# Two activation biases as immediates in place of a column in SBUF (mLSTM, then two expert layers, one core)

## The chip, the core and the metric

The kernel runs on one core of a Trainium2 chip. The metric is the device time of one execution in microseconds (us): the median of three runs of the kernel before is 632.94 us. The core has a matrix engine (TensorE, PE in the profile; its weight loads are PEld), VectorE (DVE), ScalarE (ACT), GpSimd (POOL) and SyncE (SP), which issues the DMAs. Each engine works through its own queue in order, and semaphores hold an instruction until what it reads or overwrites is ready.

## The reference

Three stages follow each other, all in float32:

```python
# 1: mLSTM, 2 batches x 8 heads, 768 steps, head size 40 (gated, stabilised recurrence)
x = y.transpose(0, 2, 1, 3).reshape(1536, 320)
# 2: layer one, 320 -> 2048 -> 320
h = x @ w_in
g = h - np.tanh(h)
x = g @ w_out
# 3: layer two, four experts, 320 -> 1024 -> 320
p = domain_probs / (domain_probs.sum(-1, keepdims=True) + 1e-9)
out = sum(p[:, e:e+1] * (np.maximum(x @ w1[e], 0) @ w2[e]) for e in range(4))
```

## The kernel before

The recurrence is computed in six chunks of 128 steps for each of the two batches, as masked score matrices. Chunk after chunk feeds layer one, whose weights arrive as 64-bit words and are converted on the chip (conv). Matrices are split in a high and a low part, so that products of float32 precision are made of several matmuls: an input product of layer one is 16 matmuls of 256 columns (L679), an output product 12 matmuls of 320 columns (L729).

Layer one has 48 steps i. Step i makes a 128 x 512 block of h in a PSUM bank (in1, mm_in), applies the activation to it (hidden1) and multiplies it into the output (out1). hidden1 is a list of eight pieces, put at different places of the order of work:

- sq: Tanh (L689) and Square (L690), both from PSUM, into t and z;
- sq2: s = (z + GA)^2 (L694), with the bias GA read from column 0 of the tile ga;
- shrink: t = h - tanh(h) on DVE (L697);
- poly: two DVE instructions (L700, L701), a polynomial in z for small h, which needs s;
- small: z = Relu(T2 - z) (L704), with T2 read from column 1 of ga; it is non-zero where h is small;
- pick: a predicated copy on DVE (L707), which takes the polynomial where z is non-zero and is the last reader of the PSUM bank;
- high (ACT, L711) and low (POOL, L715): the split of the result for the output matmuls.

Each piece runs once in a step, so L694 and L704 run 48 times each, all on 128 x 512.

The order of work is written by hand: every piece of work has a key, and run() issues the pieces by rising key. Step i of layer one has keys from 4i on. For keys under 95 (the cut, a little before step 24) only the queues of TensorE and SyncE are held to that order:

```python
with tc.manual_schedule(engines={nc.tensor.engine, nc.sync.engine}):
    ...
    run(-99, P["cut"])
with tc.manual_schedule():
    run(P["cut"], 9999)
```

There a planner, which gives instructions prices of its own, sets the order on ACT, DVE and POOL. From key 95 on all five engines keep the written order. The first 23 steps share ACT with the recurrence (att_exp, L374: eight exponentials for each chunk and batch) and the weight conversion (L189, L212). From the second half of layer one on, layer two's weights and inputs are prepared as well (conv_q, L238 to L265, and build, whose pieces are L545 to L654); layer two itself is steps of key 192 + 8m, with matmuls L671 and L729.

The tile ga is [128, 24], allocated among the constants and filled at the start by two memsets on DVE (L760, L762); between them stands the memset of gap (L761), and the first scan of the gates comes behind them on DVE.

Of the kernel before, what the change touches and what calls it, by code (L numbers as in the profile page):

```python
# [7 lines left out]
F32 = mybir.dt.float32  # L8
# [3 lines left out]
ACT = mybir.ActivationFunctionType  # L12
# [86 lines left out]
T2 = 0.0625  # L99
GA = -1.2788529396057129  # L100
# [5 lines left out]
def kernel(  # L106
# [14 lines left out]
    nc = tc.nc  # L121
    const = ctx.enter_context(tc.tile_pool(name="const", bufs=1))
# [11 lines left out]
        return ps.tile([128, 512], F32, tag=f"b{i}", name=f"b{i}")  # L134

    ident = const.tile([128, 128], F32, name="ident")
    ga = const.tile([128, 24], F32, name="ga")
    xT = [xpool.tile([128, 5, 512], F32R, tag=f"xT{i}", name=f"xT{i}") for i in range(NJ // 2)]
    gap = xpool.tile([128, 16], F32, tag="gap", name="gap")
    acc = const.tile([128, NTT, DM], F32, name="acc")  # L140
# [198 lines left out]
    def att_load(j, b):  # L339
        a = att.setdefault((j, b), {})  # L340
        a["kq"] = at.tile([128, 2, 4, 128], F32, tag="kq", name="kq")
        nc.sync.dma_start(out=a["kq"], in_=kq[j, b])

    def att_kv(j, b):
        a = att[j, b]
        a["kv"] = at.tile([128, KW + H * DV], F32, tag="kv", name="kv")
        nc.sync.dma_start(out=a["kv"], in_=kv[j, b])
# [30 lines left out]
    def first_rows(b, g):  # L378
        h = slice(4 * g, 4 * g + 4)
        nc.vector.tensor_tensor(  # L380
            out=blk[b][32:48, h, :], in0=blk[b][0:16, h, :],
            in1=g_t[:, 0:128].unsqueeze(1).to_broadcast([16, 4, 128]), op=ALU.mult,
        )

    def first_late(b, g):
        p = att.setdefault((0, b), {})["e", g] = bank(2 * b + g)
        nc.tensor.matmul(p, ident, late.unsqueeze(1).to_broadcast([128, 4, 128]), start=True, stop=False)

    def first_sum(b, g):
        nc.tensor.matmul(  # L390
            att[0, b]["e", g], rows, blk[b][:, 4 * g:4 * g + 4, :].rearrange("p h t -> p (h t)"), start=False, stop=True
        )
# [28 lines left out]
    def att_s(j, b):  # L421
        t = att[j, b]["kq"]
        ps = [abank() if j else bank(4 + 2 * b + g) for g in range(2)]
        for h in range(4):
            for g in range(2):
                nc.tensor.matmul(
                    ps[g][:, h * 128:(h + 1) * 128], t[64 * g:64 * g + PK, 0, h, :], t[64 * g:64 * g + PK, 1, h, :],
                    start=True, stop=True,
                )
        for g in range(2):  # L430
            att[j, b]["s", g] = ps[g]
# [251 lines left out]
    def hidden1(hp):  # L683
        v = {}

        def sq():
            v["z"] = ew.tile([128, 512], F32, tag="z", name="z")
            v["t"] = ew.tile([128, 512], F32, tag="t", name="t")
            nc.scalar.activation(out=v["t"], in_=hp, func=ACT.Tanh)  # L689
            nc.scalar.activation(out=v["z"], in_=hp, func=ACT.Square)  # L690

        def sq2():
            v["s"] = ew.tile([128, 512], F32, tag="s", name="s")
            nc.scalar.activation(out=v["s"], in_=v["z"], func=ACT.Square, bias=ga[:, 0:1])  # L694

        def shrink():
            nc.vector.tensor_tensor(out=v["t"], in0=hp, in1=v["t"], op=ALU.subtract)  # L697

        def poly():
            nc.vector.scalar_tensor_tensor(out=hp, in0=v["s"], scalar=GB, in1=hp, op0=ALU.add, op1=ALU.mult)  # L700
            nc.vector.scalar_tensor_tensor(out=hp, in0=hp, scalar=GC, in1=v["z"], op0=ALU.mult, op1=ALU.mult)  # L701

        def small():
            nc.scalar.activation(out=v["z"], in_=v["z"], func=ACT.Relu, scale=-1.0, bias=ga[:, 1:2])  # L704

        def pick():
            nc.vector.copy_predicated(v["t"], v["z"].bitcast(I32), hp)  # L707

        def high():
            v["gh"] = gp.tile([128, 512], F32R, tag="gh", name="gh")  # L710
            nc.scalar.activation(out=v["gh"], in_=v["t"], func=ACT.Copy)  # L711

        def low():
            v["gl"] = gp.tile([128, 512], F32R, tag="gl", name="gl")
            nc.gpsimd.tensor_tensor(out=v["gl"], in0=v["t"], in1=v["gh"].bitcast(F32), op=ALU.subtract)  # L715

        return v, (sq, sq2, shrink, poly, small, pick, high, low)

    def block2(src, tag):
# [13 lines left out]
    with tc.manual_schedule():  # L733
        nc.sync.dma_start(out=f_t, in_=fg)
        nc.sync.dma_start(out=i_t, in_=ig)
        for b in range(B):
            nc.sync.dma_start(out=blk[b][0:32], in_=c_blk[:, 8 * b:8 * b + 8])
        att_load(0, 0)
        att_load(0, 1)
        att_kv(0, 0)  # L740
        att_kv(0, 1)
        c_i0 = conv("i", 0, 0), conv("i", 0, 1)
        c_i1 = conv("i", 1)
        for f in range(2):
            c_i0[f][0]()
        nc.sync.dma_start(out=acc[:, 0:6, :], in_=og[:, 0:6, :])
        nc.sync.dma_start(out=sel, in_=c_sel)
        nc.vector.memset(late, 0.0)
        nc.gpsimd.memset(ident, 0.0)
        nc.gpsimd.affine_select(  # L750
            out=ident, in_=ident, pattern=[[-1, 128]], compare_op=ALU.not_equal, fill=1.0, base=0, channel_multiplier=1
        )
        nc.gpsimd.affine_select(
            out=late, in_=late, pattern=[[1, 128]], compare_op=ALU.is_ge, fill=NEG, base=0, channel_multiplier=-1
        )
        nc.vector.memset(rows, 0.0)
        nc.vector.memset(rows[32:48], 1.0)
        for b in range(B):
            nc.vector.memset(blk[b][32:64], 0.0)
        nc.vector.memset(ga[:, 0:1], GA)  # L760
        nc.vector.memset(gap, 0.0)  # L761
        nc.vector.memset(ga[:, 1:2], T2)  # L762
        nc.gpsimd.memset(rst, 1.0)
        nc.gpsimd.memset(rst.rearrange("p (j t) -> p j t", t=128)[:, :, 0:1], 0.0)
        for b in range(B):
            nc.gpsimd.memset(st[b], 0.0)
        nc.gpsimd.memset(egb, 0.0)
        for b, g in ((0, 0), (0, 1), (1, 0)):
            first_late(b, g)
        scan_m, log_f, log_f2, scan_g, log_i, log_i2 = gates(0, 128)  # L770
        scan_m()
        log_f()
        log_i(nc.gpsimd)
        log_f2()
        scan_g()
        log_i2(nc.vector, rows[0:16])
        for b in range(B):
            for g in range(2):
                first_rows(b, g)
        att_s(0, 0)  # L780
        for g in range(2):
            first_sum(0, g)
            first_exp(0, g)
            att_k(0, 0, (g,))
        scan_m, log_f, log_f2, scan_g, log_i, log_i2 = gates(128, S)
        scan_m()
        log_f()
        first_sum(1, 0)
        first_exp(1, 0)
        att_s(0, 1)  # L790
        att_k(0, 1, (0,))
        att_a(0, 0, 0)
        log_f2()
        att_a(0, 0, 1)
        scan_g()
        nc.sync.dma_start(out=g_d, in_=g_t)
        c_i1[0]()
        for b in range(B):
            att_gb(1, b)
        att_load(1, 0)  # L800
        att_kv(1, 0)
        c_i0[0][1]()
        c_i0[1][1]()
        first_late(1, 1)
        first_sum(1, 1)
        first_exp(1, 1)
        att_k(0, 1, (1,))
        att_a(0, 1, 0)
        c_i0[0][2]()
        c_i0[0][3]()  # L810
        att_a(0, 1, 1)
        nc.scalar.activation(out=acc[:, 0:2, :], in_=acc[:, 0:2, :], func=ACT.Sigmoid)
        c_i0[0][4]()
        nc.scalar.activation(out=acc[:, 2:6, :], in_=acc[:, 2:6, :], func=ACT.Sigmoid)
        log_i(nc.gpsimd)
        for b in range(B):
            for g in range(2):
                att_h(0, b, g)
        c_i0[1][2]()
        att_den(0, 0)  # L820
        att_gate(0, 0, nc.gpsimd)
        log_i2(nc.gpsimd)
        c_i0[1][3]()
        c_i0[1][4]()
        c_i0[0][5]()
        att_u(0, 0)
        att_x(0, 0)
        att_den(0, 1)
        att_gate(0, 1, nc.vector)
        growth()  # L830
        c_i1[1]()
        x_tr(0)
        x_split(0)
        att_x(0, 1)
        att_u(0, 1)
        biases()
        x_tr(1)
        c_i0[1][5]()
        x_split(1)
        att_mask(1, 0)  # L840
        att_mask(1, 1)
        for b in range(B):
            att_st(0, b)
        c_i2, c_o0, c_i3, c_o1 = conv("i", 2), conv("o", 0), conv("i", 3), conv("o", 1)
        c_i2[0]()
        att_load(1, 1)
        att_kv(1, 1)
        att_eg(1)
        c_o0[0]()
# [304 lines left out]
```

## Time and profile before

| | |
|---|---|
| three runs, us | 632.07, 632.94, 633.74 (median 632.94) |
| span of the profiled execution, us | 633.0 (no other time of this execution is given) |
| PE busy, us | 597.6 (94% of the span) |
| PEld busy, us | 579.7 (92%) |
| DVE busy, us | 476.4 (75%) |
| ACT busy, us | 353.1 (56%) |
| POOL busy, us | 336.6 (53%) |

The span goes from the first to the last instruction of one profiled execution. Busy time is the time in which an engine has an instruction in work; instructions of one engine overlap by a little, so the distance between two starts (the pitch) is shorter than a duration. The matrix engine's clock is given as the granted share of its full speed, 2.4 GHz: 1.00 is that level, 0.50 is 1.2 GHz.

### The profile page before, as it was taken

The page shows a single profiled execution, that of the slowest core. Times are in us where ns is not written, and L with a number is a line of the kernel's source. Part 1 is how long each engine was busy: PE and PEld are TensorE (multiplying, and loading weights), DVE is VectorE, ACT ScalarE, POOL GpSimd, SP SyncE. Part 2 cuts the span into 40 slices and gives each one's busy share as a digit, 9 for nine tenths or more (in the row PEclk, how much of TensorE's full clock was granted, in tenths as well). Part 3 has the DMA queues.
Part 4 walks back from the last instruction along what each step waited for, and adds up shares of the span by engine and source line. Part 5 has one row for each costly group of instructions (what it writes and reads, how often), then busy time and mean ns, then how long its engine had stood idle before and what let it go on. Part 6 is the DMA issues. An engine that isn't in the chain of part 4 may idle for free.

```text
span 633.0 us, 12023 instructions
## 1 busy us (share of the span) xinstructions
PE 597.6 (94%) x4505; PEld 579.7 (92%) x4505; DVE 476.4 (75%) x1011; ACT 353.1 (56%) x738; POOL 336.6 (53%) x329
## 2 busy tenths in 40 slices
PE   8695899999989999899898999999999999999997
PEld 4595899999988999898888999999999999999997
DVE  8978968899686879985777766676676766666675
ACT  3687498776788997786544454223542234432221
POOL 4666857775348876669748684304844046530000
PEclk9586798999999999999998999999999999999999
DMA  7945863743010110003000130101211011201011
GB/s 252 311 131 160 312 193 111 244 174 120 2 42 23 56 55 2 1 1 88 22 3 1 33 109 22 55 1 35 76 55 55 2 35 55 76 2 42 1 43 41
DMA packets 29602, 48.15 MB, mean 76 GB/s; under 512 B 2264, under 2 KB 20056, under 8 KB 29544
## 3 DMA queue, kind: packets, MB, share of 16 engines
q1 hardware_dynamic: 29544, 47.39, 23.2%
q8 instruction: 35, 0.57, 0.4%
q14 instruction: 23, 0.19, 0.1%
HBM read 45.31 MB, written 2.06 MB: 75 GB/s over the span
## 4 chain that ended last, share of the span: by engine, by line
PE 54%; DVE 8%; ACT 5%; issue 2%; POOL 1%; DVEq 0%; ACTq 0%; POOLq 0%
PE b L729 27%; PE b L671 23%; PE b L679 3%; DVE t L707 1%; DVE xo L638 1%; DVE t L697 1%; DVE b L987 1%; DVE s L987 1%; ACT z L690 1%; ACT gh L711 1%; POOL gl L715 1%; DVE gh L722 1%; ACT gh L721 1%; ACT z L704 1%; ACT t L689 1%
## 5 line engine op out<-in xcount | busy, mean ns | idle before, releaser
L729 PE MATMUL b<-wo,gh 128*128 128x320 f32 x960 | 201.8, 310 | 2.3 <-DVE acc L874 1.3
L729 PE MATMUL b<-wo,gl 128*128 128x320 f32 x768 | 168.4, 311 | 2.4 <-POOL gl L715 2.3
L729 PEld LDWEIGHTS b<-wo,gh 128*128 128x128 f32 x960 | 149.8, 189 | 3.4 <-ACT so L645 1.5
L729 PEld LDWEIGHTS b<-wo,gl 128*128 128x128 f32 x768 | 123.6, 190 | 3.9 <-POOL gl L715 3.9
L679 PE MATMUL b<-xT,wi 128*128 128x256 f32 x768 | 106.7, 292 | 8.9 <-ACT wi L212 4.2
L679 PEld LDWEIGHTS b<-xT,wi 128*128 128x128 f32 x768 | 99.0, 198 | 11.1 <-ACT wi L212 4.4
L721 ACT ACTIVATE gh<-b 128x256 fp32r<-128x256 f32 x96 | 36.9, 384 | 121.6 <-DVE b L987 71.0
L715 POOL TENSOR_TENSOR gl<-t,gh 128x512 fp32r<-128x512 f32 x48 | 63.1, 1314 | 57.1 <-ACT gh L711 43.6
L671 PE MATMUL b<-so,wt 128*128 128x256 f32 x560 | 90.7, 284 | 1.4 <-DVE gl L722 0.8
L987 DVE TENSOR_TENSOR b<-b,s 128x256 f32<-128x256 f32 x192 | 81.2, 423 | 2.4 <-ACT s L991 2.4
L671 PEld LDWEIGHTS b<-so,wt 128*128 128x128 f32 x560 | 80.0, 189 | 2.8 <-DVE gl L722 1.6
L721 ACT ACTIVATE gl<-b 128x256 fp32r<-128x256 f32 x96 | 36.8, 384 | 81.0 <-DVE b L987 80.9
L246 POOL TENSOR_TENSOR wb<-raw,wb 128x384 fp32r<-128x384 f32 (+1 forms) x32 | 32.6, 1018 | 82.8 <-ACT wb L238 81.3
L722 DVE SCALAR_TENSOR_TENSOR gh<-b,gh 128x256 fp32r<-128x256 f32 x96 | 40.7, 424 | 47.6 <-ACT gh L721 47.6
L722 DVE SCALAR_TENSOR_TENSOR gl<-b,gl 128x256 fp32r<-128x256 f32 x96 | 40.7, 424 | 46.0 <-ACT gl L721 46.0
L987 DVE TENSOR_TENSOR s<-b,s 128x256 f32<-128x256 f32 x144 | 58.4, 418 | 9.3 <-PE b L671 5.0
L671 PE MATMUL b<-xo,wb 128*128 128x256 f32 x400 | 65.1, 280 | 0.1
L671 PEld LDWEIGHTS b<-xo,wb 128*128 128x128 f32 x400 | 57.8, 189 | 0.4 <-DVE gl L722 0.4
L246 POOL TENSOR_TENSOR wt<-tf,wt 128x512 fp32r<-128x512 f32 (+1 forms) x32 | 41.4, 1294 | 7.5 <-ACT wt L265 5.9
L704 ACT ACTIVATE z<-z,ga 128x512 f32<-128x512 f32 x48 | 34.7, 723 | 18.9 <-DVE b L701 12.1
L697 DVE TENSOR_TENSOR t<-b,t 128x512 f32<-128x512 f32 x48 | 32.9, 686 | 15.1 <-ACT z L690 11.7
L711 ACT ACTIVATE gh<-t 128x512 fp32r<-128x512 f32 x48 | 30.3, 631 | 20.1 <-DVE t L707 19.3
(132 smaller groups left out, 1030.2 us busy)
## 6 DMA issues: line engine op xcount, KB each, us to landing
kq<-in_kq_dram SPq DMA_DIRECT2D x12, 512.0 KB
raw<-in_wb_dram SPq DMA_DIRECT2D x16, 384.0 KB
raw<-in_wa_dram SPq DMA_DIRECT2D x7, 768.0 KB
w<-g_d SPq DMA_DIRECT2D x10, 512.0 KB
raw<-in_wa_dram SPq DMA_DIRECT2D x8, 640.0 KB
raw<-in_wb_dram SPq DMA_DIRECT2D x16, 320.0 KB
kv<-in_kv_dram SPq DMA_DIRECT2D x12, 372.0 KB
raw<-in_wb_dram SPq DMA_DIRECT2D x16, 128.0 KB
```

The lines of the kernel that those rows point to most:

```text
L246: nc.gpsimd.tensor_tensor(out=o[r, k], in0=i[r, :, q], in1=o[r, 2 * q].bitcast(F32), op=ALU.subtract)
L638: nc.vector.tensor_tensor(out=o1()[r, :, 2, sl], in0=v["o"][r, 1], in1=o1()[r, :, 2, sl].bitcast(F32), op=sub)
L671: nc.tensor.matmul(o[:, 0:256], w[:, kw, b if b < 3 else b - 3], x_op(t, a, kx), start=(i == 0), stop=(i == 3),)
L679: nc.tensor.matmul(hp[:, c0:c0 + w], w_in(n, lo, kt, f), xt[:, xk, x0:x0 + w], start=(i == 0), stop=(i == 7))
L697: nc.vector.tensor_tensor(out=v["t"], in0=hp, in1=v["t"], op=ALU.subtract)
L704: nc.scalar.activation(out=v["z"], in_=v["z"], func=ACT.Relu, scale=-1.0, bias=ga[:, 1:2])
L711: nc.scalar.activation(out=v["gh"], in_=v["t"], func=ACT.Copy)
L715: nc.gpsimd.tensor_tensor(out=v["gl"], in0=v["t"], in1=v["gh"].bitcast(F32), op=ALU.subtract)
L721: nc.scalar.activation(out=g[:, 0], in_=src, func=ACT.Relu)
L722: nc.vector.scalar_tensor_tensor(out=g[:, 1], in0=src, scalar=0.0, in1=g[:, 0].bitcast(F32), op0=ALU.max, op1=ALU.subtract)
L729: nc.tensor.matmul(o[:, 0:DM], g[a][:, c:c + 128], w_out(n, lo, f), start=(first and i == 0), stop=(last and i == 2))
L987: nc.vector.tensor_tensor(out=out, in0=x, in1=y, op=ALU.add)
```

## The change

The two biases are given to the activation instructions as numbers. Nothing reads ga any more; its tile stays, named pad, and one memset of its 24 columns takes the place of the two memsets of single columns.

```diff
-    ga = const.tile([128, 24], F32, name="ga")
+    ga = const.tile([128, 24], F32, name="pad")
...
-            nc.scalar.activation(out=v["s"], in_=v["z"], func=ACT.Square, bias=ga[:, 0:1])
+            nc.scalar.activation(out=v["s"], in_=v["z"], func=ACT.Square, bias=GA)
...
-            nc.scalar.activation(out=v["z"], in_=v["z"], func=ACT.Relu, scale=-1.0, bias=ga[:, 1:2])
+            nc.scalar.activation(out=v["z"], in_=v["z"], func=ACT.Relu, scale=-1.0, bias=T2)
...
-        nc.vector.memset(ga[:, 0:1], GA)
         nc.vector.memset(gap, 0.0)
-        nc.vector.memset(ga[:, 1:2], T2)
+        nc.vector.memset(ga, 0.0)
```

## Rows read from the trace of the kernel before

**Rows 1.** The page, busy us, share of the span and instructions of each engine.
```profile
PE 597.6 (94%) x4505; PEld 579.7 (92%) x4505; DVE 476.4 (75%) x1011; ACT 353.1 (56%) x738; POOL 336.6 (53%) x329
```

**Rows 2.** Busy time by stretch; behind POOL: granted clock, DMA share, GB/s.
```profile
80.00:100.00 20.00, 18.69 (x147) 18.22 (x146) 14.20 (x32) 19.95 (x41) 11.47 (x12) 0.91 0.69 217
100.00:120.00 20.00, 20.00 (x175) 19.69 (x174) 15.02 (x33) 14.88 (x33) 16.30 (x17) 1.00 0.48 172
...
400.00:420.00 20.00, 20.00 (x155) 20.00 (x154) 13.84 (x36) 5.07 (x15) 1.41 (x2) 1.00 0.01 3
```

**Rows 3.** Groups of instructions on ACT: shapes and count, busy us, mean ns, idle before.
```profile
L704 ACT ACTIVATE z<-z,ga 128x512 f32<-128x512 f32 x48 | 34.7, 723 | 18.9 <-DVE b L701 12.1 <-DVE den L475 3.7 <-DVE den L476 3.0
L694 ACT ACTIVATE s<-z,ga 128x512 f32<-128x512 f32 x48 | 34.7, 723 | 0.3
L711 ACT ACTIVATE gh<-t 128x512 fp32r<-128x512 f32 x48 | 30.3, 631 | 20.1 <-DVE t L707 19.3 <-DVE den L475 0.9
L690 ACT ACTIVATE z<-b 128x512 f32<-128x512 f32 x48 | 28.4, 592 | 0.0
```

**Rows 4.** The timeline of ACT, 212 to 234 us: start, duration, instruction, [idle before].
```profile
212.19 0.63 ACT L711 ACTIVATE gh<-t 128x512 fp32r<-128x512 f32 x1 [0.27 <-DVE t L707]
212.72 0.58 ACT L689 ACTIVATE t<-b 128x512 f32<-128x512 f32 x1
...
213.68 0.72 ACT L704 ACTIVATE z<-z,ga 128x512 f32<-128x512 f32 x1
214.29 0.72 ACT L694 ACTIVATE s<-z,ga 128x512 f32<-128x512 f32 x1
...
228.79 0.44 ACT L545 ACTIVATE xm<-acc 128x256 f32<-128x256 f32 x1
...
233.60 0.72 ACT L694 ACTIVATE s<-z,ga 128x512 f32<-128x512 f32 x1
```

**Rows 5.** The timeline of ACT, 80 to 95 us.
```profile
81.25 0.72 ACT L694 ACTIVATE s<-z,ga 128x512 f32<-128x512 f32 x1
...
93.86 0.73 ACT L704 ACTIVATE z<-z,ga 128x512 f32<-128x512 f32 x1
94.48 0.70 ACT L374 ACTIVATE w<-w,bia 128x128 f32<-128x128 f32 x2
```

**Rows 6.** The timeline of PE: the waits that the argument uses.
```profile
95.19 1.13 PE L426 MATMUL b<-kq 64*128 64x128 f32 x14 [1.31 <-ACT w L374]
96.25 3.63 PE L679 MATMUL b<-xT,wi 128*128 128x256 f32 x16
...
186.68 2.06 PE L679 MATMUL b<-xT,wi 128*128 128x256 f32 x16 [1.58 <-DVE t L707]
...
191.91 2.05 PE L679 MATMUL b<-xT,wi 128*128 128x256 f32 x16 [1.41 <-DVE t L707]
...
229.28 0.44 PE L560 MATMUL b<-ident,xm 128*128 128x128 f32 x2 [0.42 <-ACT xm L545]
```

**Rows 7.** The timeline of ACT, 182 to 188 us.
```profile
182.24 0.73 ACT L694 ACTIVATE s<-z,ga 128x512 f32<-128x512 f32 x1
...
186.83 0.71 ACT L694 ACTIVATE s<-z,ga 128x512 f32<-128x512 f32 x1
```

**Rows 8.** The timeline of DVE, 185 to 188 us.
```profile
185.80 0.74 DVE L707 COPY_PREDICATED t<-z,b 128x512 f32<-128x512 int32 x1 [0.85 <-ACT z L704]
...
187.57 0.70 DVE L700 SCALAR_TENSOR_TENSOR b<-s,b 128x512 f32<-128x512 f32 x1 [0.47 <-ACT s L694]
```

**Rows 9.** The timeline of DVE at 234 us.
```profile
234.35 0.70 DVE L700 SCALAR_TENSOR_TENSOR b<-s,b 128x512 f32<-128x512 f32 x1
```

**Rows 10.** The timeline of DVE at the start.
```profile
3.58 0.07 DVE L761 MEMSET gap<- 128x16 f32 x1
```

**Rows 11.** Busy time in two microseconds at 96, columns as in rows 2.
```profile
96.00:98.00 2.00, 2.00 (x14) 1.88 (x12) 1.93 (x5) 2.00 (x5) 0.00 (x0) 0.61 0.69 279
```

**Rows 12.** The timeline of ACT at 30 us.
```profile
30.49 2.14 ACT L374 ACTIVATE w<-w,bia 128x128 f32<-128x128 f32 x7
```

## Prediction

> **What bounds the kernel now.** I read the busy table first, then busy time by stretches of 20 us, then the chain that ended last, and last the timelines of ACT, DVE and PE around each wait of PE that the chain or the table of waits named. The busy table says that TensorE is the bound: 597.6 of 633.0 us, while ACT, the only engine that the change makes faster, is busy for 353.1 us [rows 1]. The stretches say where this is not so. From 100 to 120 us, and again in layer two at 400, PE is busy without a gap [rows 2]; there a faster ACT can give nothing by itself. From 80 to 100 us PE is busy for 18.69 of 20 us and ACT for 19.95 [rows 2]: ACT is full, and PE waits for it. The waits of PE that matter here are few: 1.31 us at 95 us for an exponential on ACT, 1.58 and 1.41 us at 186 and 191 us for the predicated copy on DVE, 0.42 us at 229 us for a small copy on ACT [rows 6]. The chain that ended last is ACT work for most of 212 to 234 us, then DVE, and from about 335 us on matmuls alone. So the question is how much of ACT's saving lies ahead of one of these waits.
>
> **What one instruction saves.** The two touched groups, 48 instructions each, take 723 ns; the activation of the same shape from SBUF without a column operand, the copy of L711, takes 631 ns [rows 3]. The difference is 92 ns. That the function makes no large difference is suggested by the Square of L690, which takes 592 ns from PSUM with its bias a constant already [rows 3]. Instructions overlap, so what the next one gains is the pitch, not the duration: after L704 at 213.68 the next starts at 214.29, 0.61 us later; after L711 at 212.19 it starts at 212.72, 0.53 us later [rows 4]. So a follower on ACT gains 0.08 us, and a DVE instruction that waits for the end gains 0.09. I use 0.088 for one and keep 0.080 and 0.092 as its ends. The whole saving of ACT is 96 x 0.092 = 8.8 us, which is the upper bound of the change; the lower bound is nothing.
>
> It could be otherwise: were the fetch of the operand hidden behind the instruction before, nothing would come closer together inside a run of activations, and each of the three runs below would gain only at its end. That is 3 x 0.09 = 0.27 us, or 632.7 us; the two pitches speak against it. The Trainium skill (ScalarE: Activation LUTs, section "What ACT_TABLE_LOAD costs") says that back-to-back activations overlap by about 93 ns and that "each `[128,1]` pointer operand adds ≈ 93 ns", which leaves open whether the one is hidden in the other. By that, the trace agrees in size (92 ns), and its pitches, 0.61 against 0.53 us, say that it is not hidden [rows 3, 4].
>
> **Which of the 96 count.** I went through the starts on ACT from 38 to 288 us.
>
> - Before 80 us there are 10. PE waits there too, but behind weight conversion on DVE, and ACT has gaps. I count none.
> - From 80 to 95 us there are 4, from 81.25 to 93.86, in an unbroken run of ACT that ends with the exponentials PE waits for [rows 5, 6]. They start 4 x 0.088 = 0.35 us earlier. PE is full behind that [rows 2], so the gain travels with it to 180 us, where DVE, and no longer PE, sets the next wait. I take 0.20 of it, with 0 and 0.37 as ends.
> - From 95 to 180 us there are 29. PE's full queue hides them. If that cover were gone they would be worth at most 29 x 0.09 = 2.6 us.
> - From 180 to 188 us there are 4, the first at 182.24 and the last at 186.83 [rows 7]. DVE's copy at 185.80 waits 0.85 us for L704, and its polynomial at 187.57 waits 0.47 us for L694 [rows 8]; these two lead to the waits of PE at 186.68 and 191.91 [rows 6]. 4 x 0.088 = 0.35 us, ends 0.32 and 0.37.
> - From 188 to 212 us there are 12. PE alternates input and output products without a gap; I count none; uncovered, they would be worth 1.1 us.
> - From 212.7 to 234.3 us there are 12, the first at 213.68 and the last at 233.60 [rows 4]. Three of them are followed by a wait of ACT for DVE and count for nothing. Seven stand ahead of the copy at 228.79 that PE waits for [rows 4, 6], and two more ahead of the polynomial at 234.35, which starts as L694 ends [rows 4, 9]. 9 x 0.088 = 0.79 us, ends 0.72 and 0.83.
> - After 234.3 us there are 25. DVE then has work without a gap up to 251 us, and after that DVE, POOL and PE hand over to each other; ACT waits for them. I count none; uncovered, they would be worth 2.3 us.
>
> The memsets at the start: two of one column go, one of 24 columns comes. The nearest row is the memset of 16 columns, 0.07 us [rows 10]. The bounds are -0.14 and +0.07 us on DVE ahead of the first scan; I take nothing. No wait is added: L694 and L704 lose an operand that was ready long before, and no transfer is moved.
>
> **The sum.** 0.20 + 0.35 + 0.79 = 1.34 us. Against the profiled execution's 633.0 this is 631.7; that execution stands 0.06 above the median of the runs, so against the median, 632.94, it is 631.6 us. With the ends of the terms it is 631.4 to 631.9. This is 0.2%, and 0.3% (1.9 us, or 631.04) is about what a measurement of this kernel can tell from no change.
>
> **The rivals.**
>
> *More than the sum.* The 16 input matmuls at 96.25 take 3.63 us against 2.05 for the same work at 191.91 [rows 6]; the granted clock in these two microseconds is 0.61 [rows 11], that is, most of them at the lower level, 1.2 GHz. It fell right behind the wait of 1.31 us. If the exponentials come earlier and this wait shrinks, the fall may not come: 1.58 us more, or 630.0 us. If the wait goes altogether, as with a happier order of the planner, it is 1.31 more, 628.7 us. For it: the fall is at this one place, and ahead of it ACT is full. Against it: the waits of 1.58 and 1.41 us at 186 and 191 us brought no fall, so a wait of this length does not always bring one; and the sum shortens the wait by 0.35 us only.
>
> *Slower.* For keys under 95 the planner orders ACT, DVE and POOL, and with other prices for 46 or so activations it may order them otherwise. The place that would hurt is the same run from 80 to 95 us. If a group of exponentials for a later chunk, seven of them being 2.14 us [rows 12], slips ahead of the ones that PE waits for at 95.19, the full queue of PE behind that passes the loss on to the end; and a wait so much longer brings a second half-speed stretch, 1.58 us. 2.14 + 1.58 - 1.34 = +2.4, or 635.3 us. It decides from a delay of 1.34 + 1.9 = 3.2 us on. For it: the order there is not written, and ACT has no room. Against it: durations that change by an eighth (92 of 723 ns) on 96 of 738 activations leave most choices alone, and PE and SP keep their order, so a later group has no inputs earlier.
>
> *Hidden.* DVE or POOL takes over as the one that ends last at 186 and from 212 on, and PE has what it needs no earlier: a gain of 0 to 0.7, or 632.2 to 632.9. Against it: at both places DVE has gaps that end with ACT [rows 8].
>
> **How the numbers follow.** The sum has a chance of 0.42, more than the sum 0.33, slower 0.15, hidden 0.07, the same pitch as before 0.02 (632.7), and 0.01 that the numbers are put into a column again when the program is built (632.9). The sum's own range, with some slack, is 630.8 to 632.4, and 0.07 of its 0.42 lies past 631.04. Faster by over 0.3%: 0.33 + 0.07 = 0.40. Slower: 0.15, and 0.02 for a fall of the clock at a place I have not seen, 0.17. The rest is 0.43. The range reaches down to 628.7, where the whole wait at 95 is gone, and up to 634.5, which is no gain at all with a second half-speed stretch (632.94 + 1.58). Below lie some 0.07, above some 0.12.
>
> **What the profile after would show.** Right: L694 and L704 at about 631 ns, ACT busy for about 344 us; the pitch behind them at 0.53 us; PE's wait at 95 us shorter by some 0.3 us, the two waits at 186 and 191 us together shorter by about as much, the start of layer one's last outputs and everything from 335 us on earlier by 1.3 us, with the matmul part of layer two as long as before. Wrong: the names of L694 or L704 still show a second input, or 723 ns stand; the order of instructions on ACT before 180 us is another one, and PE's first gap-free stretch starts at another time by more than 1 us; the clock falls in other stretches than before; or ACT's gaps grow by what its instructions lost, while PE starts each step when it did.

## The result and the profile after

The change made the kernel slower.

| | before | after |
|---|---|---|
| median, us | 633.47 (632.07 to 635.92, 6 runs) | 638.87 (635.9 to 640.31, 6 runs) |
| ratio to before, with its 95% interval | | 1.0068 [1.0046, 1.009] |
| span of the profiled execution, us | 633.0 | 634.1 |

By the ratio, which is not the quotient of the two medians (1.0085), the loss is 0.68%, 4.3 us [2.9, 5.7]; by the medians it is 5.4 us.

Two more things are needed to read this. The device time of an execution is about 1.8 us above its span (635.9 and 634.1 for the profiled execution of after), so the profile of before stands for a run of some 634.8 us and not, as the prediction had it, of 633.0. And the profiled execution of after is the shortest of its six. Its mean granted clock was 0.970; the median over the runs of after is 0.963, over the runs of before beside the experiments 0.970. So the profile below shows where PE waits, but less of the loss than a usual run has; no usual run of after was traced.

The operand itself did what was forecast. The busy table of after, beside [rows 1]:

```profile
PE 597.0 (94%) x4505; PEld 578.6 (91%) x4505; DVE 479.2 (76%) x1010; ACT 345.8 (55%) x738; POOL 336.9 (53%) x329
```

The groups of ACT in after, beside [rows 3]; the second input is gone from the names:

```profile
L694 ACT ACTIVATE s<-z 128x512 f32<-128x512 f32 x48 | 30.4, 634 | 0.3
L711 ACT ACTIVATE gh<-t 128x512 fp32r<-128x512 f32 x48 | 30.3, 632 | 27.0 <-DVE t L707 25.9 <-DVE den L474 0.9
L704 ACT ACTIVATE z<-z 128x512 f32<-128x512 f32 x48 | 30.3, 632 | 13.9 <-DVE b L701 10.8 <-DVE den L475 2.8 <-DVE den L474 0.2
```

723 ns became 632 and 634, as long as the copy without a column. The timeline of ACT in after (start, duration), beside [rows 4]:

```profile
214.15 0.63 ACT L704 ACTIVATE z<-z 128x512 f32<-128x512 f32 x1
214.67 0.63 ACT L694 ACTIVATE s<-z 128x512 f32<-128x512 f32 x1
215.19 0.74 ACT L212 ACTIVATE wo<-raw 128x640 fp32r<-128x640 f32 x1
```

The pitch behind both is 0.52 us in place of 0.61: the whole 0.09 us reaches the next instruction, so the fetch of the column was not hidden behind the instruction before it. The Trainium skill (ScalarE: Activation LUTs, section "What ACT_TABLE_LOAD costs") prices a `[128,1]` operand at about 93 ns; the 89 to 91 ns here agree, and the pitch adds that back-to-back issue does not hide it.

What went wrong is on PE, some 20 us ahead of the first place where the prediction counted a gain. The timeline of PE in after (start, duration, instruction, [idle before <- what ended it]):

```profile
64.89 1.13 PE L426 MATMUL b<-kq 64*128 64x128 f32 x14 [1.56 <-DVE xT L521]
65.94 2.15 PE L679 MATMUL b<-xT,wi 128*128 128x256 f32 x16
...
75.87 0.42 PE L450 MATMUL b<-st,kq 104*128 104x82 f32 x2 [2.29 <-DVE w L436]
...
79.01 2.05 PE L679 MATMUL b<-xT,wi 128*128 128x256 f32 x8
...
90.87 1.17 PE L679 MATMUL b<-xT,wi 128*128 128x256 f32 x8
...
96.17 1.13 PE L426 MATMUL b<-kq 64*128 64x128 f32 x14 [0.69 <-ACT w L374]
...
101.39 1.16 PE L426 MATMUL b<-kq 64*128 64x128 f32 x14 [0.71 <-DVE w L436]
...
187.61 3.51 PE L679 MATMUL b<-xT,wi 128*128 128x256 f32 x16 [2.55 <-DVE t L707]
```

Before had no wait of PE at 76 us. Here PE stands 2.29 us for a masked product on DVE (L436, att_a), and eight input matmuls at 79.01 take 2.05 us where eight of the same kind take 1.17 at 90.87: little more than half speed. At 187 us a wait of 2.55 stands in place of before's 1.58 and 1.41 [rows 6], and the 16 matmuls behind it take 3.51 us in place of 2.06. Busy time by stretch shows the same (behind POOL: granted clock, DMA share, GB/s), first before:

```profile
72.00:76.00 4.00, 4.00 (x36) 3.69 (x36) 2.76 (x5) 3.23 (x5) 4.00 (x5) 0.93 1.04 366
76.00:80.00 4.00, 4.00 (x36) 4.00 (x36) 3.97 (x8) 0.96 (x2) 1.63 (x2) 1.00 0.23 87
80.00:84.00 4.00, 4.00 (x38) 4.00 (x36) 2.41 (x7) 3.98 (x6) 2.56 (x3) 1.00 0.95 273
```

and after:

```profile
72.00:76.00 4.00, 1.71 (x14) 1.54 (x13) 3.80 (x8) 1.51 (x3) 4.00 (x5) 1.00 1.06 363
76.00:80.00 4.00, 4.00 (x28) 4.00 (x29) 1.41 (x3) 1.30 (x2) 2.40 (x3) 0.76 0.07 26
80.00:84.00 4.00, 4.00 (x29) 4.00 (x29) 4.00 (x8) 2.85 (x4) 2.40 (x3) 0.82 0.76 256
```

PE is busy for 1.71 of the 4 us up to 76, and behind the gap it is "busy" without a break but does 28 and 29 matmuls in place of 36 and 38, at a granted clock of 0.76 and 0.82.

Why is the product late? PE and SP carry out the same instructions in the same order in both kernels. ACT, DVE and POOL do not: for keys under 95 the planner has set other places for a good number of them (by the sequences of the two traces, at least 25 instructions on ACT, 42 on DVE and 7 on POOL stand elsewhere). The timeline of DVE before,

```profile
69.86 0.67 DVE L436 TENSOR_TENSOR w<-w,b 128x512 f32<-128x512 f32 x1
70.45 1.52 DVE L200 SCALAR_TENSOR_TENSOR x<-raw,x 128x640 int32<-128x640 int32 x1
71.90 0.68 DVE L436 TENSOR_TENSOR w<-w,b 128x512 f32<-128x512 f32 x1
73.75 0.69 DVE L697 TENSOR_TENSOR t<-b,t 128x512 f32<-128x512 f32 x1 [1.18 <-ACT z L690]
74.51 0.70 DVE L700 SCALAR_TENSOR_TENSOR b<-s,b 128x512 f32<-128x512 f32 x1
75.12 1.28 DVE L436 TENSOR_TENSOR w<-w,b 128x512 f32<-128x512 f32 x2
```

and after:

```profile
67.94 0.69 DVE L436 TENSOR_TENSOR w<-w,b 128x512 f32<-128x512 f32 x1 [0.51 <-POOL kd L412]
...
70.36 1.66 DVE L200 SCALAR_TENSOR_TENSOR x<-raw,x 128x640 int32<-128x640 int32 x1
72.05 0.69 DVE L697 TENSOR_TENSOR t<-b,t 128x512 f32<-128x512 f32 x1
72.66 0.69 DVE L700 SCALAR_TENSOR_TENSOR b<-s,b 128x512 f32<-128x512 f32 x1
73.25 1.28 DVE L436 TENSOR_TENSOR w<-w,b 128x512 f32<-128x512 f32 x2
74.45 0.69 DVE L701 SCALAR_TENSOR_TENSOR b<-b,z 128x512 f32<-128x512 f32 x1
75.05 0.68 DVE L436 TENSOR_TENSOR w<-w,b 128x512 f32<-128x512 f32 x1
```

Chunk 2 has four masked products, two for each batch. Before, both of batch 0 come first, at 69.86 and 71.90. After, the second of batch 0 (heads 4 to 7) is last of the four: behind two instructions of layer one, both products of batch 1 and a third instruction of layer one. The written keys have it last as well (19.4; those of batch 1 have 19): it was in before that the planner had taken it ahead. PE's order is fixed, and batch 0 comes first in it (L450 and L455), so PE waits for the one product that was put off.

How the difference runs through the execution: the start of matmul n on PE (counted from 0) in each profiled execution, minus that of before, worked out from the traces (us; a minus is earlier; the last four columns are experiments below).

```text
n      before   after   old order,   old order,     new order,   one product
       start            numbers      late product   columns      put back
 300    61.92   +0.73    +0.10        +0.58          +2.46        +2.41
 340    72.93   -2.49    +0.68        -1.27          +1.28        +1.19
 350    73.59   -2.49    +0.68        -1.27          +1.28        +1.19
 400    79.45   +1.20    +0.68        +5.29          +3.06        +1.19
 450    85.34   +1.58    +0.68        +6.41          +3.78        +1.19
 550   100.20   -0.54    -1.10        +5.21          +1.71        -0.93
 600   105.53   +0.68    -1.10        +5.21          +7.32        +0.26
 800   129.14   +0.60    -0.08        +5.29          +6.66        -0.41
1000   152.35   +0.46    +2.79        +5.32          +7.73        +0.29
1200   177.15   +0.48    +2.81        +5.34          +7.75        +0.29
1600   233.99   +0.12    +2.13        +5.32          +7.39        -1.01
2000   290.06   -0.12    +2.12        +5.29          +7.21        -1.23
2400   352.79   +1.11    +2.61        +8.12          +7.29        +0.03
4400   615.14   +1.12    +2.65        +8.13          +7.30        +0.04
```

From 350 to 450 after loses 4.07 us: 2.29 of wait, most of the rest in the half-speed stretch. But just ahead, from 300 to 340, it had gained 3.2 us. There before waits 3.31 us and then runs at half speed:

```profile
65.90 2.04 PE L426 MATMUL b<-kq 64*128 64x128 f32 x14 [3.31 <-ACT wo L212]
67.87 3.78 PE L679 MATMUL b<-xT,wi 128*128 128x256 f32 x16
```

After waits 1.56 us there, and the same 16 matmuls take 2.15 us. So in this execution the half-speed stretch came some 10 us later and not once more, and from 300 to 450 after loses only 0.85 us net. From 450 to 550 it gets 2.1 back, since the wait at 95 is 0.69 in place of 1.31 and the half-speed stretch at 96 [rows 6, 11] does not come. It loses 1.2 again from 550 to 600, where the wait at 101 us stands, and 1.2 from 2000 to 2400, as the kernel with one product put back does. In layer two, from 2400 on, all kernels run alike, to 0.04 us. The column of the old order with numbers warns against reading single executions to a microsecond: that kernel has the order of before and a faster operand, yet lost 2.9 us from 800 to 1000, where its granted clock fell to 0.50 for a while in this execution, the slowest of its twelve.

### The profile page after: what moved, and what is told of

The parts are those of the page before. It is cut to its first block, busy times and chain, and to the rows that moved or that the text cites. A ratio compares the mean times of both kernels' runs of the same rounds, so it can differ in the third digit from the quotient of the medians.

```text
span 634.1 us, 12028 instructions
## 1 busy us (share of the span) xinstructions
PE 597.0 (94%) x4505; PEld 578.6 (91%) x4505; DVE 479.2 (76%) x1010; ACT 345.8 (55%) x738; POOL 336.9 (53%) x329
## 3 DMA queue, kind: packets, MB, share of 16 engines
HBM read 45.31 MB, written 2.06 MB: 75 GB/s over the span
## 4 chain that ended last, share of the span: by engine, by line
PE 63%; DVE 13%; ACT 8%; issue 3%; POOL 1%; DVEq 0%; ACTq 0%; POOLq 0%
PE b L729 29%; PE b L671 22%; PE b L679 6%; PE b L455 2%; DVE t L707 2%; DVE t L697 2%; DVE xo L638 1%; PE b L450 1%; ACT t L689 1%; ACT z L690 1%; DVE b L986 1%; DVE s L986 1%; PE b L426 1%; ACT gh L711 1%; POOL gl L715 1%
## 5 line engine op out<-in xcount | busy, mean ns | idle before, releaser
L707 DVE COPY_PREDICATED t<-z,b 128x512 f32<-128x512 int32 x48 | 35.8, 746 | 2.9 <-ACT z L704 2.5
```

## The experiments

Two theories were put against each other. **Order:** the loss comes from the other order that the planner makes when the 96 instructions are cheaper to it; the numbers as such gain a little. **Operand:** the loss comes from the faster instructions themselves, which shift ACT against DVE and PE. A third, **start**, puts it down to the one memset in place of two; the second and the fourth kernel below keep the two and are slow, so it falls. From the kernel with one product put back on, **place** (that one late product makes the loss) stands against **spread** (many small delays make it). Ratios are against runs of the kernel before on the same chip.

### Old order with numbers

The order is made with the columns; then, in the finished program, the operand of the 96 activations is replaced (the edit is shortened here, as are those below).

```diff
         tile_mlstm_moe_moe2_kernel(tc, *args)
+    for blk in blocks:
+        for k, i in enumerate(blk.instructions):
+            if reads_ga(i):  # 96 activations
+                v = ImmediateValue(dtype=float32, value={0: GA, 1: T2}[i.ins[1].offset])
+                blk.instructions[k] = copy.replace(i, ins=(i.ins[0], v, i.ins[2], i.ins[3]))
```

> The numbers in all 96 activations, with the instruction order of the kernel before on every engine. Order theory (what costs is the planner's new order of ACT, DVE and POOL for keys under 95): faster than before by the sum of the prediction, about 1.3 us, ratio 0.998, L694 and L704 at about 632 ns. Operand theory (the shorter activations themselves move PE's waits and bring more half-speed stretches): as slow as the changed kernel, ratio about 1.007. Start theory (one memset of 24 columns in place of two): about 1.000, as the two memsets are kept.

Measured: 632.17 us, ratio 0.998 [0.9959, 1.0]. The group of L694 (L704 has 632 ns):

```profile
L694 ACT ACTIVATE s<-z 128x512 f32<-128x512 f32 x48 | 30.4, 633 | 0.3
```

and the waits of PE in its timeline, beside [rows 6]:

```profile
95.61 1.13 PE L426 MATMUL b<-kq 64*128 64x128 f32 x14 [1.04 <-ACT w L374]
96.67 2.15 PE L679 MATMUL b<-xT,wi 128*128 128x256 f32 x16
...
189.15 2.12 PE L679 MATMUL b<-xT,wi 128*128 128x256 f32 x16 [1.58 <-DVE t L707]
...
194.28 2.12 PE L679 MATMUL b<-xT,wi 128*128 128x256 f32 x16 [1.25 <-DVE t L707]
...
231.42 0.44 PE L560 MATMUL b<-ident,xm 128*128 128x128 f32 x2 [0.28 <-ACT xm L545]
```

With the faster instructions and the old order there is no loss and no wait at 76 us. The waits that the prediction counted on are shorter by 0.27 at 95, 0 and 0.16 at 186 and 191, and 0.14 at 229.

### New order with columns

The reverse: the order of after, then columns for the numbers.

```diff
-        nc.vector.memset(ga, 0.0)
+        nc.vector.memset(ga[:, 0:1], GA)
+        nc.vector.memset(ga[:, 1:2], T2)
...
         tile_mlstm_moe_moe2_kernel(tc, *args)
+    for blk in blocks:
+        for k, i in enumerate(blk.instructions):
+            if has_number(i):  # GA or T2, 96 activations
+                blk.instructions[k] = copy.replace(i, ins=(i.ins[0], column_of(i), i.ins[2], i.ins[3]))
```

> The columns in all 96 activations, with the instruction order of the changed kernel and the two memsets of before. Order theory: slower than before by as much as the changed kernel and the lost saving together, 5 to 7 us, ratio 1.007 to 1.011. Operand theory: the time of before, ratio 1.000. Start theory: 1.000.

Measured: 641.19 us, ratio 1.0108 [1.0065, 1.0152]. One of its ACT groups, and PE's timeline:

```profile
L694 ACT ACTIVATE s<-z,pad 128x512 f32<-128x512 f32 x48 | 34.8, 725 | 0.3
```

```profile
69.15 3.78 PE L679 MATMUL b<-xT,wi 128*128 128x256 f32 x16
...
78.09 0.42 PE L450 MATMUL b<-st,kq 104*128 104x82 f32 x2 [0.73 <-DVE w L436]
...
105.26 2.07 PE L426 MATMUL b<-kq 64*128 64x128 f32 x14 [2.34 <-DVE w L436]
```

The operand is that of before, and the kernel is as slow as after or slower. With this the four combinations are there: old order 1 and 0.998, new order 1.0108 and 1.0068. The order decides. In this execution the late product costs only 0.73 us at 78, and the wait at 105, also for a masked product that stands one place later, is the larger. The granted clock was 0.58 from 80 to 84 us, right behind the first of them, and 0.57 and 0.58 from 104 to 112, at and behind the second; from matmul 550 to 600 this execution loses 5.6 us. It has the half-speed stretch at 69 us too, which the profile of after, with the same order, lacks.

### Numbers in one half of the steps

```diff
-            nc.scalar.activation(out=v["s"], in_=v["z"], func=ACT.Square, bias=ga[:, 0:1])
+            nc.scalar.activation(out=v["s"], in_=v["z"], func=ACT.Square, bias=GA if i >= 24 else ga[:, 0:1])
```

and the same for T2; i is the step of layer one. In the second half the order is written by hand, so with i >= 24 the order in the first half is exactly that of before; with i < 24 the order is that of after.

> The numbers in steps 24 to 47 alone, where the order is written; the order of the first half stays that of before. Order theory: faster by the terms that lie behind key 95 (0.35 + 0.79 us), about 1 us, ratio 0.998 to 0.999. Operand theory: half of the loss, ratio about 1.003. Start theory: 1.000.

Measured: 632.77 us, ratio 0.9976 [0.9959, 0.9993].

> The numbers in steps 0 to 23 alone; the planner's order is that of the changed kernel. Order theory: slower by the changed kernel's loss and the missing gain of the second half, 5 to 6 us, ratio 1.007 to 1.010. Operand theory: half of the loss, ratio about 1.003. Start theory: 1.000.

Measured: 639.84 us, ratio 1.0088 [1.006, 1.0116], and in PE's timeline the wait of after:

```profile
76.36 0.42 PE L450 MATMUL b<-st,kq 104*128 104x82 f32 x2 [2.29 <-DVE w L436]
```

All of the loss comes with the first half, and the second half alone gives all the gain that was measured. The version with numbers from step 24 on is the only one whose whole interval lies below before, by 0.24% [0.07%, 0.41%].

### One product put back

The change is kept as it is; only the second product of batch 0 in chunk 2 gets a key that is 2 lower. Three DVE instructions move.

```diff
-                    add(k + p["a"][c], 3, att_a, j, c // 2, c % 2)
+                    add(k + p["a"][c] + (-2 if (j, c) == (2, 1) else 0), 3, att_a, j, c // 2, c % 2)
```

> The changed kernel with the key of one piece lowered by two, the masked product of chunk 2, batch 0, heads 4 to 7, so that the planner puts it ahead of layer one's shrink and polynomial again, as before; nothing else of the order moves but two small neighbours on DVE. Place theory (this product, late on DVE, makes PE wait 2.29 us at 75 us, and the half-speed stretch behind that wait takes 1 to 1.3 us): 2.3 to 3.5 us come back, ratio to before 1.002 to 1.004. Spread theory (many small delays of the new order, no one place): under 1 us comes back, ratio 1.006 to 1.009.

Measured: 634.95 us, ratio 1.0004 [0.9986, 1.0022]; before had 634.92 on this chip. Busy time by stretch:

```profile
76.00:80.00 4.00, 4.00 (x37) 4.00 (x36) 2.34 (x5) 2.08 (x3) 3.73 (x4) 1.00 0.41 154
80.00:84.00 4.00, 4.00 (x35) 4.00 (x35) 4.00 (x7) 3.00 (x4) 2.40 (x4) 1.00 0.69 220
```

The wait is gone, the clock stays at 1.00 and PE does 37 and 35 matmuls again. Of the 0.68% that the change lost, 0.64 come back with one instruction of DVE ahead of batch 1's products again, more than the place theory expected (1.002 to 1.004); each ratio is uncertain by some 0.2%. The verdict rests on these ratios and not on the two profiles: at the end of the table they differ by only 1.1 us, and that of after is its fastest run. The wait at 101 us is still there (0.70 us).

### Two products put back

As the last, and the first product of chunk 3 one key lower, which in after stands behind one more piece of layer one and ends PE's wait at 101 us. With it 12 instructions on DVE, 7 on ACT and 3 on POOL stand elsewhere than in after.

```diff
+                    add(k + p["a"][c] + {(2, 1): -2, (3, 0): -1}.get((j, c), 0), 3, att_a, j, c // 2, c % 2)
```

> As the kernel with one product moved, and the first product of chunk 3 one key earlier too, so that chunk 3's products stand on DVE about as in the kernel before; PE's wait of 0.7 to 2.3 us at 101 us should go. Place theory: another 0.7 to 2 us, ratio to before 0.998 to 1.001. Spread theory: 1.005 to 1.008.

Measured: 634.26 us, ratio 0.9988 [0.997, 1.0007]. The wait there:

```profile
102.09 1.16 PE L426 MATMUL b<-kq 64*128 64x128 f32 x14 [0.17 <-DVE w L436]
```

It was 0.70 us in the kernel with one product put back. The step to that kernel, 0.16%, is in the expected direction, but the intervals overlap.

### Old kernel, the one product late

The kernel before with its columns; the same product is made to follow the last one of batch 1 on DVE. A few other instructions shift with it (by the traces 5 on ACT, 7 on DVE with the product, 3 on POOL). Its lines behind the edit have numbers higher by 5.

```diff
+        if (j, b, g) == (2, 0, 1):
+            tc.add_manual_dep(product, att[2, 1]["p", 1].ins.name, ...)
```

> The kernel before, with columns, and that one product of chunk 2 held behind the two of batch 1 on DVE, as in the changed kernel; the planner shifts a few more activations for it. Place theory: PE waits about 2 us more at 75 us and a half-speed stretch follows, 2.3 to 3.5 us slower, ratio 1.004 to 1.006. Spread theory: under 1 us, ratio 1.000 to 1.0015.

Measured: 641.16 us, ratio 1.0098 [1.0071, 1.0124]. The timeline of PE and the stretches:

```profile
77.99 0.69 PE L455 MATMUL b<-st,kq 104*128 104x82 f32 x2 [3.18 <-DVE w L436]
...
83.10 2.06 PE L684 MATMUL b<-xT,wi 128*128 128x256 f32 x8
```

```profile
76.00:80.00 4.00, 2.01 (x10) 2.04 (x10) 3.78 (x7) 1.67 (x3) 1.11 (x1) 0.62 0.35 131
80.00:84.00 4.00, 4.00 (x20) 4.00 (x20) 0.66 (x2) 2.77 (x2) 1.40 (x2) 0.50 0.00 0
84.00:88.00 4.00, 4.00 (x22) 4.00 (x21) 3.12 (x4) 2.78 (x5) 2.34 (x3) 0.60 0.74 256
```

So the one misplaced product, with the few that shift with it, makes the loss without any number in an activation. The size was expected too small: it is 6.2 us. The wait is 3.18 us, and behind it PE runs at half speed from 78 to about 87 us; from matmul 350 to 450 this execution loses 7.7 us, of which 4.5 are half speed (1.9 us had been gained from 300 to 340). It is the longest of its six runs, and it lost another 2.8 us from 2000 to 2400.

### One of the two numbers in the first half

Both kernels have both numbers from step 24 on. The first has in the early steps the number of small alone (L704), the second that of sq2 alone (L694).

```diff
+            nc.scalar.activation(..., func=ACT.Square, bias=GA if i >= 24 else ga[:, 0:1])   # first kernel
+            nc.scalar.activation(..., func=ACT.Relu, scale=-1.0, bias=T2)
...
+            nc.scalar.activation(..., func=ACT.Square, bias=GA)   # second kernel
+            nc.scalar.activation(..., func=ACT.Relu, scale=-1.0, bias=T2 if i >= 24 else ga[:, 1:2])
```

> Numbers in all 48 of L704, and in L694 for steps 24 to 47 alone (72 of the 96). The planner leaves the product of chunk 2 where it was, ahead of batch 1's. Place theory: no loss, a gain between nothing and 1.5 us, ratio 0.997 to 1.000; PE's wait of 2 us and more for a product on DVE near 76 us is not there. Spread theory (any new order of the planner costs): 1.003 to 1.006, since ACT, DVE and POOL still stand in another order than before at some dozens of places.

Measured: 634.63 us, ratio 1.0009 [0.9989, 1.0029], a little above the range that the place theory gave, which the interval reaches. The planner moves other instructions, but not the product, and PE's wait there is short:

```profile
74.69 0.45 PE L450 MATMUL b<-st,kq 104*128 104x82 f32 x2 [0.45 <-POOL kq L419]
```

> The reverse: numbers in all 48 of L694, and in L704 for steps 24 to 47 alone. The planner puts that product behind batch 1's, as in the changed kernel. Place theory: slower, ratio 1.005 to 1.010, with PE's wait near 76 us and a half-speed stretch behind it. Spread theory: 1.003 to 1.006, like the kernel with the two biases exchanged.

Measured: 640.68 us, ratio 1.0102 [1.0076, 1.0129]. The product is moved back, and the waits are those of after, 1.73 in place of 0.71 us at the product of chunk 3:

```profile
78.34 0.42 PE L450 MATMUL b<-st,kq 104*128 104x82 f32 x2 [2.29 <-DVE w L436]
...
106.37 1.18 PE L426 MATMUL b<-kq 64*128 64x128 f32 x14 [1.73 <-DVE w L436]
```

This execution is a usual one (641.0 us). From matmul 350 to 450 it loses 5.6 us and from 550 to 600, at chunk 3's product, 3.8. So where the product is late, chunk 3's can cost as much; but with the first alone put back the loss was gone.

A cheaper L694 in the first half is what makes the planner put the product off. L704, just as much cheaper, moves 15 instructions on ACT and 25 on DVE and costs nothing that can be measured: not every new order hurts.

## Why the prediction was wrong

**What one instruction saves: right.** 89 to 91 ns against a forecast of 92, a pitch of 0.52 against 0.53, ACT busy for 345.8 against 344 us.

**The sum, for the order of before: the size holds, its terms less well.** Old order with numbers gave 0.998 and numbers in the second half 0.9976, against 631.6 / 632.94 = 0.9979. Their intervals allow 0 to 2.6 and 0.4 to 2.6 us, so they do not confirm 1.34 us to a few tenths. The profiles suggest that the two terms from 180 to 234 us were too large: where 0.35 + 0.79 = 1.14 us was forecast, PE gained 0.68 us between matmuls 1200 and 1600 with all numbers and 0.17 with those of the second half. The copy that PE waits for at 186 us is on DVE, and that wait did not shrink at all (1.58 in both), as the rival "hidden" had it. In these two executions the half-speed stretch at 96 us did not come (16 matmuls in 2.15 and 2.16 us, [rows 6] had 3.63), as the rival "more than the sum" had it. If this is so in most runs, it made up for the terms, and that the size came out is partly luck. In the second of them the wait in front was 1.51 us, longer than the 1.31 of before, so the runs do not show that the shorter wait took it away; with a single traced execution of before, this stays open.

**The step that failed** is "Which of the 96 count", in its first item: "Before 80 us there are 10. PE waits there too, but behind weight conversion on DVE, and ACT has gaps. I count none", together with the argument that prices changed by an eighth "leave most choices alone, and PE and SP keep their order, so a later group has no inputs earlier". These instructions were looked at for what they gain when each stays in its place. The reading was loose too: the trace of before names ACT's conversion (L212) at the end of two of these waits, 4.17 us at 53 us and 3.31 at 66, and POOL's (L215) at the end of one of 1.74; they are longer than any wait that the sum counts. But under key 95 their durations are also inputs of the planner, and new prices reorder three engines. That most choices stay was true (PE and SP: all) and no comfort: one instruction of 0.69 us on DVE was enough. With the new order the ratio was 1.0108 even with columns, and with the numbers and this one instruction put back 1.0004. And that PE's order is fixed speaks for the rival and not against it: at 72 us the planner had other DVE instructions run first, and PE could not go round the one that was missing.

**The rival "slower" had the mechanism and missed place, price and chance.** A planner's choice, a wait of PE, a half-speed stretch behind it: all three came. But it was looked for where ACT is full, among the exponentials at 80 to 95 us, and it came on DVE at 72 to 75 us, an engine on which the change touches only the memsets at the start. The price of +2.4 us took in one half-speed stretch of 1.58 us; in the profiles the place cost 4.1 us (after, where 3.2 had been gained just ahead) and 7.7 us (old kernel, late product, where 1.9 had been), and by the ratio the whole change costs 4.3 us. That 4.1 and 4.3 lie so close is chance, since the profile of after ends only 1.1 us behind before's. The upper end of the range, 634.5, fell with it. Of the marks named for a wrong prediction, two show in the profile: the order under key 95 is another one, and the clock falls in other stretches.

**The memsets:** no run tried them by themselves; new order with columns and numbers in the first half keep the old ones and lose all the same. At matmul 100 after stands 0.6 us ahead of before, and old order with numbers, which has the old memsets, 0.3: a difference of single executions, from which nothing is read.

**What stays open.** How the loss of 4.3 to 5.4 us divides between waiting and half speed, and between chunk 2's product and chunk 3's, in a usual run: the granted clock of after is lower by 0.007 in the median, 0.007 x 635 = 4.4 us of full speed not granted, an estimate of the clock's part that is too high if PE stood still in some of it. Why the same late product leaves a half-speed stretch of different length. And the smaller delays of the new order, such as a wait of PE for DVE of 0.92 us at 57 us: they were not tried.

## What to carry to other kernels

Where a planner orders some engines, a cheaper instruction is a new input to the planner; before counting what it saves, list the instructions on all planned engines that stand close in front of a wait or a tight hand-over to an engine with a fixed order, and price what it costs if one of them slips behind its neighbours. To judge such a change, run it twice: with the old order kept and the new operand put in afterwards, and with the new order alone. When the order is at fault, make the change only where the order is written by hand (0.9976 here), or pin the instruction that slipped (1.0004).

## What the runs showed of the hardware that was not expected

- A wait of PE costs more than its length when the clock falls behind it. After the waits of 2.29 and 3.18 us for the product, PE did 28 and 20 matmuls in 4 us in place of 36 (granted clock 0.76 and 0.50). After 2.55 us at 187 us in after, 16 matmuls took 3.51 us; after the 1.58 and 1.25 us in old order with numbers the same 16 took 2.12.
- The fall does not follow from the length of one wait alone: it came behind 1.31 us at 95 us in before, and not behind 1.51 us there with numbers in the second half; and old order with numbers ran at 0.50 from 132 to 136 us, where before has 1.00 with the same instructions in the same order.
- The runs of one kernel differ, by 8.7 us for new order with columns (637.38 to 646.03), while its instructions are the same; the shortest of these six has a mean granted clock of 0.973, the longest 0.952.
